# A static instruction order that knows of eight DMA semaphores, with fewer small transfers, token factors in thirds and identity products at the start

## The chip, the cores and the metric

The kernel runs on one core of one Trainium2 chip. The metric is device time in microseconds (us) of one execution, given as a median over several executions. Kernels of one batch ran on the same chip, beside runs of the kernel before, and are compared with those runs only.

## The reference

```python
def rmsnorm(x, g):
    return x / np.sqrt(np.mean(x * x, axis=-1, keepdims=True) + 1e-06) * g
# q, k, v: (8 batches, 12 heads, 448 positions, 64); g_q, g_k: (64,)
scores = 1/np.sqrt(64) * rmsnorm(q, g_q) @ rmsnorm(k, g_k).transpose(0, 1, 3, 2)
attn = softmax(scores)                                    # + 1e-9 in the divisor
x = (attn @ v).transpose(0, 2, 1, 3).reshape(3584, 768)   # "tokens"
out = ((x @ w_a) * (x @ w_b)) @ w_out                     # (768,1536), (768,1536), (1536,768)
```

The three weight matrices arrive as 64-bit floats, because the inputs multiply float32 data with a numpy double. The kernel rounds them to float32, in one step on ScalarE and six on VectorE.

## The kernel before

The kernel works on 48 pairs of heads. For a pair it loads q, k and v, squares and reduces q and k, forms a power on GpSimd, transposes, multiplies to scores, takes exponentials on ScalarE, and multiplies with v. The sums of the exponentials go through DRAM and back (`few`, `inv`, `rec`), so that VectorE needs only a small reciprocal of a 112x8 tile. During the first pairs the weights come in, are rounded, and combined so that seven products of blocks do the work of eight; the same scheme needs four differences of token blocks (`x`; the prediction calls them token factors) for each two batches. `pq` is the first product of the feed-forward part.

Nothing of the order is written by hand. Each step is given to a planner with a guessed duration; at build time the planner plays the engines through and fixes the order in which each engine's instructions stand. On the chip every engine keeps that order, whatever comes late.

```python
class Plan:
    def run(self):
        ...
        def buffers(n):            # when is a buffer free? the one `bufs` openings earlier
            t, count = 0.0, {}
            for x in members(n):
                for name in ops[x][8]:
                    tag, bufs = self.tags[name]
                    had = opened.setdefault(tag, [])
                    k = len(had) + count.get(tag, 0) - bufs
                    ...
                        t = max(t, last[had[k]])
            return t
        ...
                        at[n] = max(f, ready[n], t, port if ops[n][10] else 0.0) + turn
        ...
                if ops[x][7]:      # a transfer of so many KB: when will it have landed?
                    dma[e] = max(dma[e], t) + ops[x][7] / (200.0 if dma["SP" if e == "ACT" else "ACT"] > t else 250.0)
                    end[x] = dma[e] + 2.5
```

A transfer is taken to have landed 2.5 us after its bytes would have passed at 200 to 250 GB/s. The loads, the weights and the token differences:

```python
    def load_gains():              # six transfers of 256 bytes
        for n, g in enumerate((g_q, g_k)):
            for e in range(2):
                nc.sync.dma_start(gain[e * D:(e + 1) * D, n:n + 1], g.rearrange("(d o) -> d o", o=1))
            nc.sync.dma_start(grow[:, n], g.rearrange("(o d) -> o d", o=1))
...
                    for e in range(2):         # k: two transfers, q and v: one each
                        nc.sync.dma_start(x[:, :, e], src[b, h0 + e].rearrange("(p j) d -> p j d", j=NJ))
...
                        nc.scalar.dma_start(to, moe_w_out[k * P:(k + 1) * P, :])   # ScalarE's queue
...
            op("SP", 0.8, p - 3.0, spread_out, [t], [few], new=[few], kb=20)
            op("DVE", 0.25, p - 3.0, lambda: nc.vector.reciprocal(fews[0], fews[0]), [], [few])
            op("SP", 0.4, p - 3.0, leave, [few], [f"inv{p}"], kb=20)
            op("SP", 0.8, p - 3.0, come_back, [f"inv{p}"], [t], kb=230)
...
                    nc.vector.tensor_tensor(quads[to], quads[x], quads[y], ALU.subtract)   # whole blocks
```

## Time and profile before

| | kernel before |
|---|---|
| first three runs | 1649.41 us median (1646.23 to 1649.55) |
| span of the profiled run | 1643.6 us |
| first scores | 20.42 us |
| first feed-forward product | 186.62 us |
| from there to the end | 1643.6 - 186.62 = 1456.98 us |

The three last rows divide the span at two events.

The timeline around the longest gap of TensorE (PE) in the kernel before; the columns are start, duration, engine, line, operation, and in brackets the idle time before and what ended it:

```profile
286.87 1.13 SPq L597 DMA_DIRECT2D rec<-inv  x2
...
290.95 0.62 DVE L626 TENSOR_TENSOR x<-x,rec 128x448 f32<-128x448 f32 x1 [5.18 <-DMA rec<-inv]
...
292.16 6.19 PE L776 MATMUL pq<-x,st 128*128 128x448 f32 x10 [4.81 <-DVE hT L814]
```

The reciprocals come back too late for their place in VectorE's order, VectorE stands for 5.18 us, and PE then idles for 4.81.

### The profile page before, as it was taken

The numbers are of one execution on the slowest core, as the hardware profiler recorded it, in microseconds if no ns is written. First come the engines' busy times: TensorE is split into PE (matmuls) and PEld (weight loads), VectorE is DVE, ScalarE is ACT, GpSimd is POOL, SyncE is SP. The second block draws the span as 40 slices with busy tenths as digits, with TensorE's granted clock in tenths as the row PEclk, the third lists the DMA queues.
The fourth block names the chain that finished last, engine by engine and source line by source line (L and its number), as shares of the span: only waits on it lengthen the run. The fifth ranks groups of instructions, "written<-read, shape, count | busy, mean of one in ns | idle before, by whom it ended". The sixth has DMA issues, their size and how long they took to land.

```text
span 1643.6 us, 14865 instructions
## 1 busy us (share of the span) xinstructions
PE 1590.1 (97%) x5448; PEld 770.9 (47%) x5448; DVE 723.9 (44%) x960; ACT 432.5 (26%) x776; POOL 405.6 (25%) x200
## 2 busy tenths in 40 slices
PE   5898899899999999999999999999999999999998
PEld 2333344444444455555444455555544555555554
DVE  5786657689565621122266551122235422222331
ACT  5666554111365520000255530000034000000000
POOL 3222446101364620100264640000133000100000
PEclk9999999999999999999999999999999999999999
DMA  6676425254333443222232433322222342222131
GB/s 210 220 235 200 133 78 180 94 204 173 120 99 115 119 126 120 101 75 93 80 98 80 118 113 120 106 79 89 96 69 77 115 135 101 91 77 91 62 112 50
DMA packets 132742, 191.19 MB, mean 116 GB/s; under 512 B 63284, under 2 KB 121396, under 8 KB 122932
## 3 DMA queue, kind: packets, MB, share of 16 engines
q1 hardware_dynamic: 104916, 137.06, 26.3%
q10 hardware_dynamic: 27744, 53.09, 8.9%
q8 instruction: 45, 0.74, 0.2%
q14 instruction: 37, 0.30, 0.1%
HBM read 154.01 MB, written 35.94 MB: 116 GB/s over the span
## 4 chain that ended last, share of the span: by engine, by line
PE 85%; DVE 5%; DMA 5%; ACT 1%; issue 1%; SPq 1%; POOL 1%; ACTq 0%; DVEq 0%; POOLq 0%
PE pq L776 44%; PE po L704 23%; PE sc L508 7%; PE o L529 7%; PE su L564 2%; PE pt L488 2%; DMA few<-rec 2%; DMA k_sb<-in_k_dram 2%; DMA inv<-few 1%; POOL ms L455 1%; DMA rec<-inv 1%; DVE ms L444 1%; DVE st L378 1%; SPq L418 0%; DVE x L640 0%
## 5 line engine op out<-in xcount | busy, mean ns | idle before, releaser
L776 PE MATMUL pq<-x,st 128*128 128x448 f32 x2016 | 769.7, 542 | 5.4 <-DVE hT L814 4.8
L776 PEld LDWEIGHTS pq<-x,st 128*128 128x128 f32 x2016 | 381.5, 191 | 382.4 <-issue 368.4
L514 ACT ACTIVATE ET<-sc,ms 112x448 f32<-112x448 f32 x384 | 216.1, 636 | 126.7 <-PE sc L508 111.5
L704 PE MATMUL po<-st,hT 128*128 128x384 f32 x744 | 247.5, 488 | 0.0
L455 POOL TENSOR_TENSOR ms<-ms,expo 112x16 f32<-112x16 f32 x48 | 152.2, 3171 | 241.1 <-DVE ms L451 219.2
L544 POOL TENSOR_TENSOR sum<-sum,ET 112x896 f32<-112x896 f32 x72 | 165.0, 2292 | 150.7 <-DVE sum L542 145.9
L824 POOL TENSOR_TENSOR hT<-hT,t 128x448 f32<-128x448 f32 x24 | 28.6, 1190 | 688.3 <-DVE t L822 688.3
L508 PE MATMUL sc<-qkT 64*112 64x448 f32 x768 | 175.7, 575 | 20.7 <-ACT ET L514 11.2
L704 PEld LDWEIGHTS po<-st,hT 128*128 128x128 f32 x744 | 139.3, 190 | 102.6 <-issue 8.8
L529 PE MATMUL o<-ET,v_sb 112*64 112x448 f32 x768 | 166.6, 556 | 0.9 <-ACT x L622 0.9
L704 PE MATMUL po<-st,fin 128*128 128x384 f32 x432 | 144.6, 489 | 0.0
L798 ACT COPY hT<-pq 128x448 f32<-128x448 f32 x24 | 12.8, 531 | 417.0 <-PE pq L776 417.0
L508 PEld LDWEIGHTS sc<-qkT 64*112 64x112 f32 x768 | 61.5, 176 | 115.1 <-issue 78.0
L704 PEld LDWEIGHTS po<-st,fin 128*128 128x128 f32 x432 | 80.6, 190 | 58.8 <-issue 3.5
L529 PEld LDWEIGHTS o<-ET,v_sb 112*64 112x64 f32 x768 | 50.5, 138 | 105.5 <-issue 100.4
L444 DVE TENSOR_REDUCE ms<-sq 112x8 f32<-112x512 f32 x96 | 64.8, 675 | 63.8 <-ACT sq L437 57.1
L724 DVE TENSOR_TENSOR o_sb<-fin,po 128x384 f32<-128x384 f32 x56 | 30.9, 553 | 138.2 <-PE po L704 138.2
L459 DVE TENSOR_TENSOR qn<-q_sb,ms 112x512 f32<-112x512 f32 x48 | 67.9, 1415 | 23.2 <-PE pt L488 11.2
L836 POOL TENSOR_TENSOR hT<-hT,t 128x448 f32<-128x448 f32 x48 | 59.8, 1246 | 44.7 <-DVE t L833 44.7
L542 DVE TENSOR_TENSOR sum<-ET 112x896 f32<-112x896 f32 x36 | 39.9, 1108 | 66.9 <-PE su L564 63.8
L829 DVE TENSOR_TENSOR hT<-U,pq 128x448 f32<-128x448 f32 x48 | 29.8, 621 | 74.5 <-PE pq L776 74.5
L801 ACT COPY t<-pq 128x448 f32<-128x448 f32 x24 | 12.8, 533 | 186.6 <-PE pq L776 186.6
(66 smaller groups left out, 929.7 us busy)
## 6 DMA issues: line engine op xcount, KB each, us to landing
st<-kept SPq DMA_DIRECT2D x36, 1344.0 KB
st<-kept_o SPq DMA_DIRECT2D x28, 1152.0 KB
kept<-st ACTq DMA_DIRECT2D x12, 1344.0 KB
q_sb<-in_q_dram SPq DMA_DIRECT2D x48, 224.0 KB
k_sb<-in_k_dram SPq DMA_DIRECT2D x96, 112.0 KB
v_sb<-in_v_dram SPq DMA_DIRECT2D x48, 224.0 KB
rec<-inv SPq DMA_DIRECT2D x88, 112.0 KB
kept_o<-st ACTq DMA_DIRECT2D x6, 1344.0 KB
```

Of the source, the lines that this page charges most:

```text
L444: nc.vector.tensor_reduce(rs[p][:, s], xs["sq", nm, p], AX, ALU.add)
L455: nc.gpsimd.tensor_tensor(msf, msf, expo, ALU.pow)
L459: nc.vector.tensor_tensor(qns[p].rearrange("p j h d -> p h j d"), xs["q", p].rearrange("p h (j d) -> p h j d", d=D), rs[p][:, 0].rearrange ...
L488: nc.tensor.transpose(t[:, j * SP:(j + 1) * SP], x[:, j].rearrange("p h d -> p (h d)"), ident[0:SP, 0:SP])
L508: nc.tensor.matmul(t[:, e, 0:S], lhsT=qkTs[p][rows, 1, c * SP:(c + 1) * SP], rhs=qkTs[p][rows, 0, :], start=True, stop=True)
L514: nc.scalar.activation(E[:, e], scs[p, c][:, e, 0:S], AF.Exp, scale=rs[p][:, 1, 2 * c + e:2 * c + e + 1])
L529: nc.tensor.matmul(os_[p][e * D:(e + 1) * D, :], lhsT=xs["v", p][:, e, c * D:(c + 1) * D], rhs=ETs[p, c][:, e], start=(c == 0), stop=(c == ...
L542: nc.vector.tensor_tensor(sums[p], ETs[p, 0], ETs[p, 1], ALU.add)
L544: two[ADD_UP].tensor_tensor(sums[p], sums[p], ETs[p, c], ALU.add)
L704: nc.tensor.matmul(held["po"][:, 0:HALF], lhsT=a[0]()[:, c], rhs=sts[beta, 12 + place_of[f]][:, c], start=(c == 0), stop=(c == MH - 1))
L776: nc.tensor.matmul(banks[bank][:, 0:S], lhsT=sts[at][:, f, c * P:(c + 1) * P], rhs=quads[x][:, c], start=(start and c == 0), stop=(stop an ...
L836: lambda i=i, n=n, nm=nm: two[TIMES].tensor_tensor(C(i, n), C(i, n), held[nm], ALU.mult), [t], [hp[i]],
```

## The change

The intent: let the planner know that a transfer must wait for the semaphore of the transfer eight places earlier (a semaphore is the counter on which an instruction waits until a transfer has landed; the compiled program has eight of them for the transfers of SP and ScalarE and takes them in turn), spend fewer transfers, make the token differences as soon as their parts are there, and keep TensorE busy until the first pair. The buffer rule is also new: any free buffer of a kind, not only the next in turn. The core of the diff:

```diff
+    LANES = 8
...
-                    k = len(had) + count.get(tag, 0) - bufs
+                    had = opened.setdefault(tag, [None] * bufs)
+                    since = [(last.get(o, 0.0), k) for k, o in enumerate(had) if (tag, k) not in taken.values() and not left.get(o)]
...
-                        at[n] = max(f, ready[n], t, port if ops[n][10] else 0.0) + turn
+                        at[n] = max(f, ready[n], t, port if ops[n][10] else 0.0,
+                                    sent[ops[n][11] - 1 - self.LANES] if ops[n][11] else 0.0) + turn
...
                     end[x] = dma[e] + 2.5
+                    sent += [end[x]] * ops[x][11]
...
-            for e in range(2):
-                nc.sync.dma_start(gain[e * D:(e + 1) * D, n:n + 1], g.rearrange("(d o) -> d o", o=1))
             nc.sync.dma_start(grow[:, n], g.rearrange("(o d) -> o d", o=1))
...
-                    for e in range(2):
-                        nc.sync.dma_start(x[:, :, e], src[b, h0 + e].rearrange("(p j) d -> p j d", j=NJ))
+                    nc.sync.dma_start(x, src[b, h0:h0 + 2].rearrange("h (p j) d -> p j h d", j=NJ))
...
-                    nc.vector.tensor_tensor(quads[to], quads[x], quads[y], ALU.subtract)
+                    nc.vector.tensor_tensor(quads[to][:, c], quads[x][:, c], quads[y][:, c], ALU.subtract)
...
+        def warm():
+            for x in range(4):
+                nc.tensor.matmul(warms[0][:, 0:P], lhsT=ident, rhs=ident, start=True, stop=True)
...
+                spread_gains()      # one small product puts the gains into 128 partitions
+                for x in range(WARM):      # WARM = 12
+                    op("PE", 0.86, 1e6, warm, ["warm"], ["warm"], mode="full")
...
+                if (p - 1) % (2 * HP) >= 2 * HP - KH:
+                    combine((p - 1) // (2 * HP), (p - 1) % KH)
```

## The prediction

> **What bounds the kernel now.** I read the engine totals first, then busy time by stretches of the span, then the list of waits, then the timeline around each gap of TensorE.
>
> ```profile
> span 1643.6 us, 14865 instructions
> PE 1590.1 (97%) x5448; PEld 770.9 (47%) x5448; DVE 723.9 (44%) x960; ACT 432.5 (26%) x776; POOL 405.6 (25%) x200
> ```
>
> TensorE (PE) is busy for all but 53.5 us of 1643.6. The change leaves its real work as it is, so it can only win idle time, or work that ran slowly. Busy time by stretches (columns: stretch, length, busy time of each engine with its count, granted clock, DMA share, GB/s) tells where that lies:
>
> ```profile
> 0.00:20.42 20.42, 1.99 (x8) 1.33 (x8) 4.36 (x11) 5.11 (x9) 3.80 (x10) 1.00 0.80 236
> 20.42:186.62 166.20, 147.09 (x721) 55.16 (x721) 121.19 (x161) 109.40 (x193) 54.34 (x16) 0.95 0.67 212
> 186.62:205.00 18.38, 15.44 (x60) 6.22 (x59) 13.35 (x13) 8.35 (x17) 8.85 (x5) 0.91 0.18 50
> 205.00:410.00 205.00, 198.19 (x626) 92.61 (x625) 153.72 (x180) 61.35 (x95) 58.72 (x29) 0.98 0.42 145
> 410.00:1637.50 1227.50, 1227.38 (x4040) 615.56 (x4038) 430.86 (x597) 248.24 (x465) 279.92 (x143) 1.00 0.30 98
> 1637.50:1643.60 6.10, 0.00 (x0) 0.00 (x0) 0.47 (x1) 0.00 (x0) 0.00 (x0) 0.82 0.12 38
> ```
>
> From 410 to 1637.5 us PE idles 0.1 us: three quarters of the kernel can't be helped. The last 6.1 us are the last output transfer. So everything is in the first 410 us: 18.4 idle before the first scores, 19.1 until the first feed-forward product at 186.62, 2.9 around it, 6.8 until 410. Together 47.3 us.
>
> The timeline shows what the early gaps are. First the start, then one gap of the attention stage:
>
> ```profile
> 5.38 0.34 ACTq L365 DMA_DIRECT2D hraw<-in_moe_w_out_dram  x1
> 7.00 4.17 ACTq L365 DMA_DIRECT2D hraw<-in_moe_w_out_dram  x2
> 11.21 0.63 ACT L437 ACTIVATE sq<-q_sb 112x512 f32<-112x512 f32 x1 [8.87 <-DMA gain<-in_g_k_dram]
> 20.42 3.26 PE L508 MATMUL sc<-qkT 64*112 64x448 f32 x8 [1.37 <-ACT qkT L495]
> 24.64 1.76 PE L508 MATMUL sc<-qkT 64*112 64x448 f32 x8
> ...
> 133.62 0.38 ACTq L368 DMA_DIRECT2D hraw<-in_moe_w_a_dram  x1
> 134.04 0.63 ACT L514 ACTIVATE ET<-sc,ms 112x448 f32<-112x448 f32 x1 [6.20 <-DMA rec<-inv]
> 135.26 1.84 PE L508 MATMUL sc<-qkT 64*112 64x448 f32 x4 [4.38 <-ACT ET L514]
> ```
>
> ScalarE (ACT) issues the weight loads from its own queue, in order with its arithmetic. Its first square needs only q, yet starts when a 256-byte gain load has landed; an exponential whose input is ready waits for a load of reciprocals. Neither reads these. What links them is the transfer semaphore: in the compiled program of before, every transfer takes the next of eight semaphores and first waits for the transfer eight places earlier. A weight load thus stops ACT until an unrelated transfer lands, and PE after it. The old planner does not know this.
>
> A second cost: after a gap PE is slow. The same eight score products take 3.26 us at 20.42 and 1.76 us at 24.64.
>
> **What the Trainium skill says.** (1) "TensorE: Matmul & The Clock Gate", Part 1: The HAM clock gate: TensorE starts at half clock, and about 3.4 us of idleness brings it back. The trace agrees on the size: 3.26 against 1.76 us, 0.98 against 0.60 for four k transposes; though a gap of 3.2 us (41.5 to 44.69) already led to 3.33 us for eight score products. (2) "DMA: Bandwidth & Descriptors", Queues, rings and completion order: each transfer engine alternates between queues packet by packet, so a small transfer beside large ones is late. It agrees: k of the second pair, issued at 8.17 and 8.82 beside weight loads of 768 KB, landed at 18.68 us, 9.86 after the second issue. (3) The same page, Anatomy of one DMA: semaphore waits happen on the issuing sequencer. The trace agrees, with ACT's 8.87 and 6.20 us above.
>
> **The change part by part.**
>
> *Start.* Six gain loads become two and two k loads one, so nine SP transfers before v become four, and no early weight load should queue behind a gain load. The second weight load, on q's semaphore, went out at 5.38, so q had landed then. ACT could square at 5.4 instead of 11.21: 5.8 us. From the square to the first scores it is 20.42 - 11.21 = 9.2 us (two squares, two reductions, a 2.96 us power on GpSimd, the q multiplication, four transposes, one scaled copy), all still needed, so scores near 14.6. But weight loads let out earlier compete with k (896 runs of 256 bytes, as before), and the second pair's k landed only at 18.68. Of 5.8 I count 5.
>
> *Identity products.* Twelve groups of four with lowest priority, in PE's idle time before the first `values` product. If the clock is up by then, the first scores save 3.26 - 1.76 = 1.5 us and the q transposes 1.01 - 0.60 = 0.4: 1.9 us.
>
> *Order that knows the eight semaphores.* The gaps that a weight load's wait on ACT caused, with the slow products behind them (against 1.76 for eight score and 1.72 for eight value products): at 44.69, 3.20 idle + 1.57 + 1.39 = 6.2; at 84.50, 2.41 + 1.20 + 0.45 = 4.1; at 135.26, 4.38 + 0.83 (1.84 against 1.01) + 1.23 (2.95 against 1.72) = 6.4. Sum 16.7. One k load instead of two also makes 8 transfers per pair from 9 (q, v, one inv, two each of few and rec). The planner reckons a transfer as its bytes at 200 to 250 GB/s plus 2.5 us. The trace has 7.21 us for 3.5 KB of inv at 58.21, so it still believes that semaphores come free too early. I count 60%: 10.
>
> *Thirds.* The four token-factor subtractions block VectorE at the switch to the feed-forward part:
>
> ```profile
> 185.79 7.59 DVE L640 TENSOR_TENSOR x<-x 128x1344 f32<-128x1344 f32 x4
> 196.18 0.60 PE L488 MATMUL pt<-ident,k_sb 112*128 112x112 f32 x4 [2.94 <-ACT ET L514]
> 197.00 4.13 PE L776 MATMUL pq<-x,st 128*128 128x448 f32 x6
> ```
>
> In thirds, eight of twelve are done before; four of about 0.63 us (my estimate from 0.62 for a 128x448 VectorE product) stay, 2.5 us instead of 7.6. The gap with its slow products costs 2.94 + 4.13 - 2.52 = 4.6 us; I count 3.5. Later rounds sit under a full PE: nothing.
>
> *Other reordering.* The remaining gaps up to 205 us sum to about 9 (twelve of 0.16 to 1.25 us); those up to 410, with the slow products after 292.16, to another 9. The largest is 4.81 at 292.16, VectorE waiting for rec, which the semaphores don't explain. New slot and semaphore rules shuffle these, both ways: 3.
>
> *Costs.* One product and one copy for the gains, before the first scaled copy; the PE queue may stand at an identity product or at the gain product when k is ready: 1. Twelve small subtractions instead of four large add 12 x 0.63 - 6.5 = 1 us of VectorE per round, hidden.
>
> Sum: 5 + 1.9 + 10 + 3.5 + 3 - 1 = 22.4 us; 1649.4 - 22.4 = 1627.
>
> **The rivals.**
> (a) *The waits only move.* The planner's transfer times are too short beside 212 GB/s of traffic, so ACT stops at other places, and SP, also in order, holds loads back. For it: small transfers of 6.5 to 7.2 us on the path. Against it: a model with semaphores can hardly be worse than none, and there are fewer transfers. Only start, warm-up and thirds stay: about 10 us, 1639.
> (b) *VectorE becomes the bound of the first stage.* It is busy 121.2 of 166.2 us while rounding weights. With 30 us less it would be at 89%, in chains of 10 us for one set of weights that delay the small steps of q and k. Also, rounding still to do is pushed into the 205 to 410 stage, where it is at 75%. Some gain made before 186 us would be given back: 12 us in all, 1637.
> (c) *Nearly everything is won.* Ceiling: 47.3 idle + 2.3 slow at the start + 10.6 slow later (2.96, 1.65, 2.06, 1.61, and 2.3 after 292.16) = 60 us, less a start of some 13 us that stays (my estimate: q at 5.4 and the 9.2 us chain, a little shortened): 47. With 85% of this, 40 us: 1609. It would need the stage to fit all engines closely.
> (d) *The new slot rule misjudges* which buffer comes free, and the static order puts a product too early: PE is in order, so each costs microseconds. As only the first 410 us have slack on other engines, a bad order after 410 would show as new gaps: up to +10, 1655. Little speaks for it.
>
> **Range and chances.** Most weight lies between (a) or (b) and my sum: 1612 to 1642 eight times in ten. Faster by over 2% means below 1616.4, that is 33 of the 47 us that can be won at all: 0.14. Slower by over 2% needs 33 us of new gaps in a stage where PE is now full: 0.01. The rest, 0.85.
>
> **What would show it.** Start: the first square near 5.5 to 7 us, first scores near 14 to 16 us and lasting 1.8 us, not 3.3. Order: ACT's waits put down to transfers it does not read (24.1 us up to 205 us: 8.9, 6.2, 5.5, 3.5) fall by more than half, and the granted clock from 20 to 187 us rises from 0.95. Thirds: no block of four subtractions over 5 us, first feed-forward product 15 to 20 us earlier than 186.6. From 410 us on no new idle time. I am wrong if q lands much later than 5.4 us beside more weight loads, if first scores come early but the first feed-forward product doesn't (then VectorE or transfers bound the stage), or if PE's idle time after the start stays near 29 us.

## More of the kernel before

The prediction shows the stages. First, what VectorE (DVE) waited for up to 410 us in the kernel before, transfers alone; the columns are the waiting instruction, the transfer, the sum in us, how often, and the longest:

```profile
DVE x L626 <- DMA rec<-inv: 24.8, 8, 5.3
DVE few L600 <- DMA few<-rec: 15.8, 7, 6.3
```

Together 40.6 us. Both instructions are short, but VectorE keeps its order, so rounding and reductions stand behind them.

## The result, and the profile after

The changed kernel took 1647.95 us (median of 6 runs, 1643.5 to 1654.08), the kernel before 1647.53 us (median of 6, 1644.69 to 1649.55). The ratio is 1.0005, with a 95% interval of 0.9982 to 1.0029: the same. Ratios here are the mean time of one kernel's runs over that of the other's of the same rounds, so they aren't quite the ratios of the medians. The result lies outside the predicted range.

The profile fell on the slowest of the six runs (1654.08 us), so its span of 1652.2 us is not typical; a second profile of the same program (after_again, 1646.3 us) stands beside it:

| us | before | after | after, again |
|---|---|---|---|
| start to first scores | 20.42 | 21.75 | 18.46 |
| first scores to first feed-forward product | 166.20 | 174.33 | 175.54 |
| from there to the end | 1456.98 | 1456.12 | 1452.30 |
| span | 1643.6 | 1652.2 | 1646.3 |

The attention stage, which should have become shorter, is 8 to 9 us longer. A part of that comes back later. Totals of the changed kernel:

```profile
span 1652.2 us, 15068 instructions
...
PE 1604.7 (97%) x5546; PEld 786.7 (48%) x5546; DVE 729.3 (44%) x992; ACT 432.7 (26%) x777; POOL 401.8 (24%) x200
```

PE is busy 14.6 us longer than before (1604.7 against 1590.1), but the identity products, 15.7 us in all, are more than that. It is idle for 47.5 us in place of 53.5 only because they fill the start: from 20.42 to 1637.5 us its idle time grew, from 29.0 to 36.2 us (33.6 in after_again). Busy time by stretches of the changed kernel, in the columns that the prediction explains:

```profile
20.42:186.62 166.20, 139.87 (x679) 52.18 (x680) 117.72 (x159) 105.03 (x184) 46.97 (x13) 0.94 0.65 208
186.62:205.00 18.38, 15.18 (x73) 5.74 (x70) 15.31 (x19) 10.12 (x19) 9.24 (x4) 1.00 0.22 63
205.00:410.00 205.00, 201.78 (x646) 94.51 (x645) 153.96 (x181) 66.53 (x105) 61.17 (x31) 0.98 0.42 143
410.00:1637.50 1227.50, 1224.01 (x4028) 613.96 (x4028) 438.40 (x623) 247.55 (x465) 280.62 (x144) 1.00 0.30 98
```

PE is busy 7.2 us less between 20.42 and 186.62 (139.87 against 147.09), 3.6 us more from 205 to 410, and 3.4 us less in the long stretch behind, where the kernel before had no idle time. Every engine did less in the attention stage, and so did the transfers: it isn't that one of them filled up.

The start in the timeline of the changed kernel:

```profile
0.81 0.88 ACTq L364 DMA_DIRECT2D hraw<-in_moe_w_out_dram  x2
...
8.93 0.82 ACTq L364 DMA_DIRECT2D hraw<-in_moe_w_out_dram  x2
9.80 0.63 ACT L435 ACTIVATE sq<-q_sb 112x512 f32<-112x512 f32 x1 [7.35 <-DMA k_sb<-in_k_dram]
...
12.03 7.66 PE L868 MATMUL warm<-ident 128*128 128x128 f32 x40
...
21.75 1.76 PE L506 MATMUL sc<-qkT 64*112 64x448 f32 x8 [1.29 <-ACT qkT L493]
```

The first square, of q, still waits for a transfer that it doesn't read: the third weight load in ScalarE's queue now stands behind k, whose own landing is late beside two weight loads let out at 0.81 us. In this run the identity products (40 records, five groups, 1.53 us a group where the planner has 0.86) also kept PE until the transposes at 19.52; the granted clock between 12.03 and 19.50 us was 0.59. In after_again it was 1.00 from 11.67 to 16.20, a group took 0.95 us, and the transposes began at 16.24. The scores then run at full speed: 1.76 us for eight.

The hold by an unrelated transfer that the change was to remove is still found, at another place:

```profile
112.95 0.37 ACTq L367 DMA_DIRECT2D hraw<-in_moe_w_b_dram  x1
113.43 1.16 ACT L512 ACTIVATE ET<-sc,ms 112x448 f32<-112x448 f32 x2 [4.49 <-DMA kept_o<-st]
...
114.64 1.01 PE L506 MATMUL sc<-qkT 64*112 64x448 f32 x4 [2.12 <-ACT ET L512]
```

And a wait for an instruction's own data, late:

```profile
88.20 0.32 SPq L419 DMA_DIRECT2D q_sb<-in_q_dram  x1
...
96.27 0.63 ACT L435 ACTIVATE sq<-q_sb 112x512 f32<-112x512 f32 x1 [4.94 <-DMA q_sb<-in_q_dram]
...
98.96 2.83 PE L506 MATMUL sc<-qkT 64*112 64x448 f32 x8 [2.53 <-ACT ET L512]
```

Q landed about 8 us after its issue. The planner gives it its 230 KB at 200 to 250 GB/s and 2.5 us, that is 3.4 to 3.7. Adding up every wait of ScalarE for a transfer up to 205 us, as the profile puts it down, with those for a tile that the instruction reads (own) apart from the others: before 10.1 own and 24.1 others; after 14.7 and 16.6; after_again 21.1 and 17.0. The sum went from 34.3 to 31.2 and 38.1.

VectorE's waits for transfers up to 410 us in the changed kernel:

```profile
DVE x L624 <- DMA rec<-inv: 22.1, 7, 4.6
DVE few L598 <- DMA few<-rec: 20.8, 6, 6.8
```

They are about as long as before (42.9 against 40.6 us; 44.6 in after_again, where one wait is put down to v). The token differences in thirds:

```profile
180.38 2.60 DVE L643 TENSOR_TENSOR x<-x 128x448 f32<-128x448 f32 x4
...
197.95 2.60 DVE L643 TENSOR_TENSOR x<-x 128x448 f32<-128x448 f32 x4
```

They are short as foreseen, but in this profile a gap of 2.04 us at 204.73 with six feed-forward products of 4.13 us behind it stays. (In after_again it is gone; a gap of 1.95 us stands at 189.00, before the first feed-forward product.) In later rounds they make gaps that did not exist, as here:

```profile
516.50 0.61 DVE L624 TENSOR_TENSOR x<-x,su 128x448 f32<-128x448 f32 x1
...
517.25 0.97 PE L562 MATMUL su<-sum,ones 112*64 112x448 f32 x4 [2.21 <-DVE x L624]
```

Before this, VectorE had worked at four of the small subtractions for 4.37 us from 508.00. A second gap of this kind, 1.28 us, stands at 896.03. Together they are the 3.5 us that PE lacks after 410.

### The profile page after: what moved, and what is told of

It is laid out like the page before. It is cut to its first block, busy times and chain, and to the rows that moved or that the text cites. A ratio compares the mean times of both kernels' runs of the same rounds, so it can differ in the third digit from the quotient of the medians.

```text
span 1652.2 us, 15068 instructions
## 1 busy us (share of the span) xinstructions
PE 1604.7 (97%) x5546; PEld 786.7 (48%) x5546; DVE 729.3 (44%) x992; ACT 432.7 (26%) x777; POOL 401.8 (24%) x200
## 4 chain that ended last, share of the span: by engine, by line
PE 83%; DMA 7%; DVE 6%; issue 1%; ACT 1%; POOL 1%; SPq 1%; ACTq 0%; DVEq 0%; POOLq 0%
PE pq L779 43%; PE po L707 23%; PE sc L506 6%; PE o L527 6%; DMA inv<-few 2%; PE su L562 2%; DMA few<-rec 2%; PE pt L486 2%; DMA rec<-inv 1%; DVE x L643 1%; DMA k_sb<-in_k_dram 1%; DVE st L377 1%; POOL ms L453 1%; DVE st L277 1%; DVE su L572 1%
## 5 line engine op out<-in xcount | busy, mean ns | idle before, releaser
L457 DVE TENSOR_TENSOR qn<-q_sb,ms 112x512 f32<-112x512 f32 x48 | 62.6, 1304 | 22.2 <-POOL ms L453 11.2
L836 DVE TENSOR_TENSOR t<-U,pq 128x448 f32<-128x448 f32 x48 | 29.6, 620 | 65.0 <-PE pq L779 63.9
```

What stands on the lines that cost most here:

```text
L457: nc.vector.tensor_tensor(qns[p].rearrange("p j h d -> p h j d"), xs["q", p].rearrange("p h (j d) -> p h j d", d=D), rs[p][:, 0].rearrange ...
```

## The experiments

Eighteen kernels ran, in five batches. A ratio is to the kernel before in the same batch. Every output was correct except where it says that it was wrong.

### 1. The start and ScalarE's queue

**after_again** is the changed kernel itself.

> The changed kernel once more, for a second profile and as the base of this call. Both theories: 1648 us, within 4 us, ratio to before 0.998 to 1.003. The first profile was the slowest of its runs (1654.08). If its single gaps (3.5 us at 66.95, 5.24 at 179.51) are set by where transfers land, some of them will be of another size here, with the same instruction order.

Measured: 1647.18 us, ratio 1.0004 (0.9983 to 1.0024). The result stands.

**fewer_warm** leaves out four of the twelve identity groups without changing the order.

```diff
-                    op("PE", 0.86, 1e6, warm, ["warm"], ["warm"], mode="full")
+                    op("PE", 0.86, 1e6, warm if x < 8 else None, ["warm"], ["warm"], mode="full")
```

> The same plan and order, but only 8 of the 12 groups of identity products are issued. Theory W (the identity products stand in PE's queue before the first transposes, as a group takes 1.15 to 1.53 us and not the 0.86 planned): the transposes start near 16.6 us instead of 19.5, first scores near 19 instead of 21.75, and the whole is 2 to 3 us faster. Rival (the start is not passed on to the rest of the stage): first scores near 19, time unchanged within 1 us.

Measured: 1649.79 us, ratio 1.0014 (0.9989 to 1.0039); first scores at 18.51 us, as in after_again. Theory W was wrong: PE now idled for 3.31 us before the transposes of q at 16.75, and the first ten score products took 4.25 us. The last groups neither help nor hurt the total within the noise.

**start_clear** lets the first four weight loads go only after the squares of the first pair.

```diff
-                if p == GATES[x]:
+                if p and p == GATES[x]:
...
+                if p == 0:      # behind normalize(0); and warm only for x < 7
+                    for x, n in enumerate(seq):
+                        if GATES[x] == 0:
+                            factors(n, x * 1.1 + 0.5, x < 8, ["sqk0"])
```

> The changed kernel, but its first four weight loads are issued from ACT only after the two squares of the first pair, and 7 of the 12 groups of identity products are issued. Theory S (at the start, early weight loads delay k from 6.7 to 8.9 us and hold ACT by k's semaphore until 9.8): q squared before 5.5 us, first scores near 13 to 15 us instead of 18.5 to 21.8. If the start is worth what the prediction said, the whole is 4 to 7 us faster than the changed kernel, near 1641. Rival R (the stage then waits for the weights, that come some 6 us later, or for the second and third pair): first scores at 13 to 15 us and the whole unchanged within 2 us.

Measured: 1656.60 us, ratio 1.0068 (1.0049 to 1.0087). From the timeline of start_clear:

```profile
3.30 0.63 ACT L435 ACTIVATE sq<-q_sb 112x512 f32<-112x512 f32 x1 [0.85 <-DMA q_sb<-in_q_dram]
...
13.52 5.04 PE L506 MATMUL sc<-qkT 64*112 64x448 f32 x16 [1.60 <-ACT qkT L493]
...
34.92 1.84 PE L506 MATMUL sc<-qkT 64*112 64x448 f32 x4 [1.27 <-ACT qkT L493]
```

Without weight traffic q is there at 3.30 us, and the first scores come at 13.52, even earlier than I had predicted. But the second pair's scores come at 34.92, where the kernel before has them at 30.81. The lead of 7 us on the first pair is lost by the second, whose reductions (25.49 and 27.75) and multiplication with q (31.89) stand in VectorE's order behind rounding steps that begin at 19.03 us; in the kernel before the reductions (17.91 and 19.45) come first and the rounding begins at 21.87. As the edit also delays the weights and makes a new order, it doesn't tell what an earlier start alone is worth.

**loads_on_pool** issues weight loads and stores from GpSimd in the same planned places; four such lines change.

```diff
-                    nc.scalar.dma_start(kept[n], sts[n].rearrange("p a b -> p (a b)"))
+                    nc.gpsimd.dma_start(kept[n], sts[n].rearrange("p a b -> p (a b)"))
```

> Same plan, but weight loads and stores are issued from GpSimd, which has its own eight semaphores, so ACT never waits for one. Theory L (the remaining loss is ACT held by a semaphore of an unrelated transfer): the ACT waits for transfers that it does not read (7.35, 4.49 and 4.71 us in the changed kernel) are gone, first scores before 20 us, 8 to 12 us faster, near 1638. Rival D (the loss is now mostly data that lands late, as SP is held in order behind small transfers of 6 to 8 us): gaps of PE stay, 0 to 4 us faster. Rival V (VectorE bounds the stage): no change.

Measured: 1656.52 us, ratio 1.0063 (1.0044 to 1.0082), first feed-forward product at 196.87 us against 194.00 in after_again. ScalarE's waits for other transfers are gone up to 205 us, those for its own data are 28.1 us (21.1 in after_again). Taking the first kind off ScalarE didn't help. As GpSimd keeps its order too, the run can't tell whether the holds were harmless or only moved.

### 2. How much is transfers, how much VectorE

**small_loads** (changed kernel) and **before_small_loads** (kernel before) load an eighth of the weights' bytes; the rest is set to 1.0 at the start, so the result is wrong.

```diff
+            nc.vector.memset(hold["h"].bitcast(FP32), 1.0)
+            nc.gpsimd.memset(hold["l"].bitcast(FP32), 1.0)
...
-                        nc.scalar.dma_start(to, moe_w_out[k * P:(k + 1) * P, :])
+                        nc.scalar.dma_start(to[:, 0:NW // 8], moe_w_out[k * P:(k + 1) * P, 0:NW // 8])
```

> Wrong result on purpose: each weight load moves an eighth of its bytes, in the same order, the rest is set once to 1.0. Theories L and D together (all lost time of the stage up to 196 us comes from transfers that land later than the plan takes them to): few, inv and k land within 4 us, PE's gaps between 22 and 196 us fall from 26 us to under 8, first feed-forward product near 172 us instead of 196, the whole near 1625. Rival V (VectorE, or the plan itself, bounds the stage): first feed-forward product after 188 us, the whole above 1640.

> Wrong result on purpose: the kernel before, with weight loads of an eighth of their bytes. Theory M2 (late transfers beside the weight traffic bound the attention stage in both kernels): from first scores to first feed-forward product 150 to 158 us instead of 166.2, and the whole 5 to 12 us below before although its start is held by setting the words. Rival (only the new plan suffers from late transfers): stage 164 to 168 us.

Measured: 1634.48 us, ratio 0.9932 (0.9913 to 0.9952), and 1629.26 us, ratio 0.9888 (0.9873 to 0.9904), although setting the words delayed the first scores to 25.02 and 23.03 us. From first scores to first feed-forward product it is 157.9 and 153.4 us, some 17 and 13 us less than with full loads. Transfers beside the weight traffic cost both kernels time. In the stage the new one gains more, in the total the old one ((1 - 0.9888) x 1647 = 18 us against (1.0004 - 0.9932) x 1647 = 12). Small_loads came out between its two expectations: the first feed-forward product is at 182.90 us.

**less_rounding** keeps the order of the changed kernel and doesn't issue three of the six VectorE steps of rounding, 3.7 us for each set of weights (wrong).

```diff
+                emit = None if at in (1, 2, 3) else emit
```

> Wrong result on purpose: the changed kernel in the same order without three of the seven rounding steps (3.7 us of VectorE for each set of weights, some 25 us up to the first feed-forward product). Rival V (VectorE bounds the stage): that product 15 to 25 us earlier than 194 to 196, the whole 12 us faster or more. Theory M2: at most 5 us earlier, the whole within 4 us of the changed kernel.

Measured: 1648.35 us, ratio 1.0017 (0.9994 to 1.0041). The first feed-forward product comes at 190.06, some 4 us earlier than in after_again, and the total doesn't move. VectorE's amount of work doesn't bound the kernel in this order.

### 3. The semaphore rule, alone and taken away

**semaphores_off** is the changed kernel with `LANES = 4000`, so that no transfer is planned to wait for another's semaphore. **old_rules** is the changed kernel with the old `run()`, so with the old buffer rule as well (the hunks of `run()` in the change, reversed). **before_semaphores_only** is the kernel before with the semaphore rule; **before_and_semaphores** has the buffer rule too.

```diff
-    LANES = 8                    # semaphores_off
+    LANES = 4000
...
-                        at[n] = max(f, ready[n], t, port if ops[n][10] else 0.0) + turn      # before_semaphores_only
+                        at[n] = max(f, ready[n], t, port if ops[n][10] else 0.0,
+                                    sent[ops[n][11] - 1 - self.LANES] if ops[n][11] else 0.0) + turn
...
+                    sent += [end[x]] * ops[x][11]
```

> The changed kernel, but the planner's eight semaphores are made 4000, so it plans as if none were ever short. Theory K (knowing the semaphores helps, and other parts of the change lose it again): 5 to 10 us slower than the changed kernel, near 1655, with more ACT waits for transfers that ACT does not read. Theory M (the planner takes every transfer to land after its bytes and 2.5 us, real ones take 6 to 8 us, so knowing which semaphore is next is worth nothing): within 3 us of the changed kernel.

> All of the change but the planner's rules: k in one transfer, two gain loads, thirds, identity products, planned by the planner of before. Theory N (the two new rules cost some 7 us, as they did on the kernel before, and the other parts gain the same): 5 to 8 us faster than the changed kernel and than before, near 1640. Rival P (every re-plan lands anywhere within some 8 us, as the static order meets late transfers in another place; no part has a fixed worth): anything from 1640 to 1655, not the sum.

> The kernel before with the semaphore rule alone (old rule for buffers). Theory N with the cost in the semaphore rule: 1651 to 1656. With the cost in the buffer rule: 1644 to 1648. Rival P: either.

> The kernel before with the planner's new rules alone (eight semaphores, buffer that came free first), its transfers as before. Theory K: 5 to 10 us faster than before, near 1638, without the ACT holds of 6.2, 3.5 and 2.9 us. Theory M: within 3 us of before, old holds gone, new ones elsewhere.

| kernel | median us | ratio (95%) |
|---|---|---|
| semaphores_off | 1648.13 | 1.0002 (0.9982 to 1.0023) |
| old_rules | 1646.72 | 1.0000 (0.9982 to 1.0019) |
| before_semaphores_only | 1658.63 | 1.0079 (1.0058 to 1.0100) |
| before_and_semaphores | 1654.31 | 1.0042 (1.0025 to 1.0059) |

In the changed kernel the rule is worth nothing. Added to the kernel before it costs 13 us (0.0079 x 1647); with the buffer rule beside it 7 (0.0042 x 1647), so the buffer rule wins back some 6 there, and nothing in the changed kernel (semaphores_off against old_rules). The profile of before_semaphores_only is 13.9 us longer than that of before: 6.3 up to the first scores, 5.4 in the attention stage, 2.3 behind it. Its first scores come at 26.68 us, because q's square stands behind the weight loads:

```profile
13.74 0.63 ACT L440 ACTIVATE sq<-q_sb 112x512 f32<-112x512 f32 x1 [11.40 <-DMA hraw<-in_moe_w_out_dram]
```

In semaphores_off ScalarE waits for transfers only 17.3 us up to 205, less than half of after_again's 38.1, and the time is the same. So the sum of these waits is not what sets the end. VectorE's waits for transfers up to 205 us hardly moved (27.3 against 30.8 us).

### 4. Thirds and k in one transfer

**whole_combine** is the changed kernel with the token differences whole again; **whole_old_rules** is the same with the old `run()`. **k_in_two** is the changed kernel with k in two transfers.

```diff
-                    nc.vector.tensor_tensor(quads[to][:, c], quads[x][:, c], quads[y][:, c], ALU.subtract)
+                    nc.vector.tensor_tensor(quads[to], quads[x], quads[y], ALU.subtract)
...
-                if (p - 1) % (2 * HP) >= 2 * HP - KH:
+                if (p - 1) % (2 * HP) == 2 * HP - 1:
...
-                    nc.sync.dma_start(x, src[b, h0:h0 + 2].rearrange("h (p j) d -> p j h d", j=NJ))      # k_in_two
+                    for e in range(2):
+                        nc.sync.dma_start(x[:, :, e], src[b, h0 + e].rearrange("(p j) d -> p j d", j=NJ))
```

> The changed kernel with the token factors whole again. If thirds are worth the 3.5 us of the prediction: 3 to 4 us slower, near 1651, and a VectorE block of over 7 us in front of the first feed-forward products. If the two gaps of PE after 410 us (2.2 and 1.3 us, VectorE at the sums) come with the thirds, these are gone, and the net is 0 to 1 us slower.

> All of the change but the planner's rules and the thirds. If thirds cost 3 to 5 us whatever the rules: 3 to 5 us faster than old_rules, ratio near 0.997. If the fall of whole_combine came from its new plan: ratio 1.000 or more. In either case no gap of PE from 410 to 1630 us.

> The changed kernel with k in two transfers again, and planned so. If one transfer for k is worth something (one semaphore fewer per pair, 0.6 us less of SP): 2 to 6 us slower than the changed kernel, near 1651. If k's time is that of its 896 runs of 256 bytes beside the weights: within 2 us. Rival P: anything within 8 us.

Measured: whole_combine 1641.96 us, ratio 0.9971 (0.9954 to 0.9988); whole_old_rules 1643.77 us, ratio 0.9978 (0.9964 to 0.9991); k_in_two 1652.24 us, ratio 1.0038 (1.0020 to 1.0055). Thirds cost (1.0004 - 0.9971) x 1647 = 5 us under the new rules and (1.0000 - 0.9978) x 1647 = 4 us under the old; the intervals of each of these pairs overlap a little. The two gaps (at 497 to 518 and 877 to 898 us) stand in all eleven profiles with thirds and in none of the nine with whole differences. Slow_transfers and slow_whole in the next part are a third such pair, with intervals apart: (0.9991 - 0.9953) x 1647 = 6 us. One transfer for k gains about 6 us (1.0038 against 1.0004) under the new rules, with intervals that overlap by a little.

### 5. The landing time that the planner assumes

**slow_transfers** (the changed kernel), **slow_whole** (with whole differences), **slow_whole_off** (as slow_whole, with `LANES = 4000`) and **before_slow** (the kernel before) change one number, up to 300 us of planned time:

```diff
-                    end[x] = dma[e] + 2.5
+                    end[x] = dma[e] + (6.0 if t < 300.0 else 2.5)
```

> The changed kernel, but up to 300 us of its plan the planner reckons 6.0 us to landing instead of 2.5. Theory M: the order fits what happens, attention stage (first scores to first feed-forward product) shrinks from 175 us to under 168, whole 5 to 10 us faster, near 1639. Rival X (transfers land late because they are late on the wire beside the weight traffic, whatever the order): the stage stays at 172 to 178 us and the whole within 3 us of the changed kernel.

> The changed kernel with whole token factors and with 6.0 us to landing in the plan up to 300 us. Theory M2 (the plan's error is its 2.5 us to landing; thirds cost 3.5 us after 410): the gains add, some 2.5 + 5 us against the changed kernel, ratio to before near 0.996, 1639 us, first feed-forward product near 187 us, no gap of PE after 410 us. The planner's own reckoning, no measurement, puts that product at 170 us for the changed kernel and at 193 here. Rival P (each re-plan lands anywhere within 8 us): ratio anywhere from 0.997 to 1.005.

> The kernel before with 6.0 us to landing in its plan up to 300 us, and nothing of the change. If the longer time alone does it: 1640 us or less, ratio under 0.997. If it needs the semaphore rule or the other parts: ratio 0.998 to 1.003, with weight loads still holding ACT (15 us or more of ACT waits for transfers that it does not read up to 205 us, where before has 24.1).

> slow_whole (1638.75 us, ratio 0.9953) planned without the eight semaphores. Theory M3 (the semaphore rule pays once the time to landing is right): slower than slow_whole by 3 us or more, ratio 0.997 to 1.001, with ACT held by transfers that it does not read (4 us or more up to 200 us, where slow_whole has 1.6). Rival (the longer time to landing does it alone): ratio within 0.0015 of 0.9953.

| kernel | median us | ratio (95%) | first scores to first feed-forward product | from there to the end |
|---|---|---|---|---|
| slow_transfers | 1644.48 | 0.9991 (0.9974 to 1.0009) | 169.88 | 1452.21 |
| slow_whole | 1638.75 | 0.9953 (0.9940 to 0.9967) | 169.42 | 1448.26 |
| before_slow | 1635.13 | 0.9924 (0.9910 to 0.9938) | 164.70 | 1449.07 |
| slow_whole_off | 1628.70 | 0.9883 (0.9867 to 0.9899) | 157.05 | 1449.55 |

One number in the kernel before, and nothing of the change, gains 12 us. With the fewer transfers, the identity products and the buffer rule of the change, whole differences and no semaphore rule, it is 18.5 us (1647.24 to 1628.70). That version beats both kernels, though both expectations for it had said that it would not beat slow_whole. A pair near it shows the number's worth without the semaphore rule once more: from whole_old_rules to slow_whole_off it is (0.9978 - 0.9883) x 1647 = 16 us, the buffer rule included. What the number does is to be seen in VectorE's waits for transfers up to 410 us, first before_slow, then slow_whole_off:

```profile
DVE few L600 <- DMA few<-rec: 5.0, 4, 2.0
DVE x L626 <- DMA rec<-inv: 0.2, 1, 0.2
```

```profile
DVE few L598 <- DMA few<-rec: 3.3, 3, 2.1
DVE x L624 <- DMA rec<-inv: 1.0, 1, 1.0
```

From 40.6 us to about 5, while ScalarE's waits for transfers up to 205 us went only from 34.3 to 28.0 us in before_slow. In before_slow the gap of 4.81 us at 292.16 is gone, and PE works 204.65 us between 205 and 410 (before 198.19); nearly all of its gain lies after the first feed-forward product (1449.07 against 1456.98 us). Slow_whole_off gains as much there and 9 us in the attention stage besides. The stretch of the attention stage in slow_whole_off, to be held against 139.87 us of PE and a clock of 0.94 in the changed kernel:

```profile
20.42:186.62 166.20, 148.04 (x746) 56.75 (x742) 128.86 (x167) 111.61 (x197) 56.05 (x17) 0.98 0.68 215
```

ScalarE's waits for unrelated transfers are still 22.1 us up to 205 in slow_whole_off, near the 24.1 of before. Those for its own data are 2.1.

With the semaphore rule the same number is worth much less: 2 us with thirds (1.0004 to 0.9991), 3 us with whole differences (0.9971 to 0.9953), both within overlapping intervals and short of the 5 to 10 us expected of slow_transfers. The rule itself costs (0.9953 - 0.9883) x 1647 = 11.5 us here. Yet VectorE's waits up to 410 us fell in slow_whole too, from 44.4 us in whole_combine to 9.0; this is the one line left:

```profile
DVE few L598 <- DMA few<-rec: 9.0, 2, 6.3
```

And before_semaphores_only, 13 us slower than the kernel before, has 33.0 us of them against 40.6. So shorter waits of VectorE don't bring the 12 us by themselves. That the number brings them is measured; that VectorE's waits are the path is shown only for the gap at 292.16 us and argued for the rest. In slow_whole unrelated transfers hold ScalarE for only 9.2 us, most of it at the start, but it waits 12.2 us for its own data (2.1 in slow_whole_off). The worst case in slow_whole's timeline:

```profile
102.28 0.66 SPq L419 DMA_DIRECT2D q_sb<-in_q_dram  x1
...
109.00 0.63 ACT L435 ACTIVATE sq<-q_sb 112x512 f32<-112x512 f32 x1 [7.70 <-DMA q_sb<-in_q_dram]
...
109.69 1.01 PE L486 MATMUL pt<-ident,qn 112*128 112x112 f32 x4 [6.65 <-DVE qn L457]
```

The load of q is issued only at 102.28 and takes 6.7 us. It came too late into SP's order, and PE idles for 6.65 us.

## Why the prediction was wrong

**"Order that knows the eight semaphores ... I count 60%: 10."** This step failed. In the changed kernel the rule brought 0 (1.0002 without it, 1.0004 with it); added to the kernel before it cost 13 us (7 with the buffer rule), and beside the longer landing time 11.5. The waits that I had summed were real, and those for unrelated transfers became fewer (24.1 to 16.6 us), but waits for late q and k took their place (10.1 to 14.7 and 21.1 us), as rival (a) has it. Nor does their sum set the time: without the rule, semaphores_off has 17.3 us of both kinds and is no faster, and slow_whole_off is the fastest of all with 22.1 us of the unrelated kind. My argument against that rival, that a model with semaphores can hardly be worse than none, is refuted by before_semaphores_only. What the kernel before did lose stood in the same paragraph of the prediction: the planner's landing time is too short. I took it for a discount of 40% on the gain. The runs show that it was a gain of its own: corrected alone, it is worth 12 us in the kernel before. It doesn't explain why the rule brought nothing, as with the longer time the rule cost no less; that stays open. And the waits that it removes are less ScalarE's than VectorE's, for `few` and `rec`, which I had not summed at all; how much of the 12 us comes by them is not shown, as slow_whole lost as many of them and gained 3.

**"Start ... Of 5.8 I count 5."** The gain loads no longer hold the square, as said, but another transfer does, and the size is off. The first square came at 9.80 us, not 5.4 (before 11.21), because the earlier weight loads delay k (held back, in start_clear, they left k there by 4.72) and ScalarE then stands behind k's semaphore. I had named that risk and charged 0.8 us for it. First scores came 1.3 us later in one profile and 2.0 earlier in the other, not 5.8 earlier. An early start is no gain by itself: start_clear had first scores at 13.52 and its total was still 10.5 us longer than that of after_again ((1.0068 - 1.0004) x 1647). But that edit also delays the weights, so what the lead alone would be worth stays open.

**"Identity products ... 1.9 us."** The effect on the first scores is as predicted (1.76 us), but in the one profile that I show the products themselves, at a granted clock of 0.59, held the transposes back until 19.52. No run takes them out altogether, so their worth in the total isn't measured.

**"Thirds ... I count 3.5. Later rounds sit under a full PE: nothing."** Wrong in sign. The gap at the switch stayed in the first profile (2.04 us), the second has one of 1.95 us before the switch, and later rounds show two gaps of 2.21 and 1.28 us, as VectorE makes the small subtractions just before a product's input. Measured cost: 4 to 6 us. PE was full there because the order fitted, not because there was room.

**"Other reordering ... 3"** and **"Costs ... 1"**. Between the first feed-forward product and the end the changed kernel is 0.9 us shorter in one profile and 4.7 in the other, the gaps of the thirds included; so up to some 4 to 8 us were won there. One transfer for k, which I had counted only as a help to the semaphores, measures 6 us. These gains, no run isolating the first, pay for the thirds and the longer attention stage, and the sum comes out at nothing.

**Rivals.** (a) is nearest in mechanism; its 1639 failed as start, warm-up and thirds didn't stay either. (b), VectorE as the bound, falls with less_rounding. (c) is excluded by the result. (d) sent me to look for new gaps after 410; there are two, and they come with the thirds, not with the buffer rule.

**The signs named.** Of those for the order none came: ScalarE's unrelated waits fell by a third, not by half, and the clock from 20 to 187 us went from 0.95 to 0.94. Of those for the thirds, the block over 5 us is gone, but the first feed-forward product came 7.4 and 9.5 us later instead of 15 to 20 earlier, and there is new idle time after 410. I had said that I'd be wrong if PE's idle time after the start stayed near 29 us: it rose to 36.2 and 33.6. Another sign of being wrong, that first scores come early and the first product doesn't, is what start_clear shows, with its late weights.

**What stays open.** Why planning with true semaphores makes orders worse. With the rule on, ScalarE's waits for its own data up to 205 us are 10.6 to 28.1 us in ten of the twelve profiles with full weight loads (3.8 in slow_transfers, 9.9 in k_in_two); with it off, 1.7 to 10.1 in six. That fits a planner that puts q and k behind semaphores that it thinks busy and issues them late, but no run isolates it, and as semaphores_off shows, fewer such waits need not mean less time. Nor is it isolated why the attention stage became longer: it is 174.3 us in whole_combine, with the new rules and without thirds, 167.6 in whole_old_rules, with neither. Also, each edit makes a whole new order, so single ratios carry some luck of the new order. The thirds' cost and the landing time's gain without the semaphore rule were each seen in two settings or more; the 6 us of k_in_two and the 1628.70 us of slow_whole_off rest on one order each, and 6.0 is the one value tried on the chip.

## What to carry to other kernels

An order fixed at build time is only as good as its assumed times: before adding a finer rule, compare the assumed landing of each kind of transfer with the trace, and correct that first. Sum the waits of every engine that keeps its order, not only of the one whose gap is easiest to explain; a 0.2 us instruction that waits for a late transfer stops all the work behind it. Try the parts of a change alone, because a part that seems only able to help (finer pieces, a truer rule) may cost time where the rest already fitted.

## What the Trainium skill lacked or had wrong

- "DMA: Bandwidth & Descriptors", Anatomy of one DMA: the fit of 2.0 us plus bytes at 436 GB/s, given for transfers issued by GpSimd, would make 224 KB take an estimated 2.5 us. Issued by SP beside weight loads, q took 8.1 us (88.20 to 96.27) and 6.7 us (102.28 to 109.00). The fit has no term for other traffic. The planner's own guess, 3.4 to 3.7 us for such a transfer, fell short in the same way, and a longer one was worth 12 us in the kernel before.
- "TensorE: Matmul & The Clock Gate", Part 1: The HAM clock gate: about 3.4 us of idleness is said to bring half clock. Here eight score products took 2.83 us, in place of 1.76, after a gap of 2.53 us, at a granted clock of 0.69 (99 to 102 us); in after_again 2.45 us after a gap of 1.95. So a shorter gap can cost too; no run tells where the limit lies.
- No page that I read tells what reusing eight transfer semaphores costs: a weight load held ScalarE's square of q for 7.35 us until k had landed, and for 11.40 us in before_semaphores_only.
